# Attention and MLP on one core: five DMA transposes and two sets of masks change their place in the order of the work

## The chip, the cores and the metric

The kernel runs on one core of one Trainium2 chip. The metric is the device time of one execution in microseconds. The kernel before takes 355.95 us (median of three runs, 355.69 to 356.04). The work of each engine is written down in one order by the program, so an edit that only moves lines changes in which order an engine meets its instructions, and what a queue of DMAs issues first.

## The reference

For each of 8 batches and 8 heads, 576 queries attend to 16 beacon keys and to the 576 keys up to their own position (head size 64). The result, with the heads side by side, is x, 576 x 512 per batch. A mixer follows: a low-rank product over the sequence is added to x, and an MLP with ReLU (512 to 2048 to 512) is added to that.

```python
scores = scale * np.matmul(q, k_all.transpose(0, 1, 3, 2))
causal[:, Nb:] = np.triu(np.ones((S, S), dtype=bool), k=1)
a = np.exp(scores - scores.max(-1, keepdims=True))
x = np.matmul(a / a.sum(-1, keepdims=True), v_all)     # heads side by side
h = x.transpose(0, 2, 1) @ U @ V
u = x + h.transpose(0, 2, 1)
out = u + np.maximum(u @ w_ch1, 0.0) @ w_ch2
```

## The kernel before

Batches are counted from 0 in the code: batch 3 is the fourth, batch 5 the sixth. Two heads make a pair, four pairs a batch; pairs are numbered p = 0 to 31, with b = p // 4 the batch and c = p % 4 the pair in it. `P6` is 16, the first pair of batch 4, and `DT0` is 4.

*Attention.* For a pair, TensorE multiplies transposed keys and queries (`kT`, `qT`) into scores in four groups of columns, each a PSUM bank per head (`visit`, line 379 from batch 4 on, line 345 before). ScalarE takes the exponential of each bank into an SBUF tile `expt`. `masks_of` lets VectorE zero what lies above the diagonal: four instructions a pair, lines 321 and 323. `av_unit` then multiplies by the values (line 394) and VectorE divides by the row sums into `xb` (lines 402 and 403). There are eight PSUM banks, taken in the order in which they were given back.

*Transposes.* For batches 0 to 3, TensorE transposes q and k. From batch 4 on, `load_whole(b)` loads them by token with 11 DMAs on GpSimd's queue (line 643, the beacons by line 199), and `turns(b)` makes a list of ten DMA transposes on SyncE's queue (line 655), in the order k0, q0, k1, q1, k2, q2, k3, q3, k4, q4 of the five tiles of tokens. `fill_turns` issues the next n of such a list. `load_batch` loads the values from batch 4 on. The tiles of batch 5 for loaded and for transposed q and k take the places of those of batch 3.

*The mixer and the MLP.* When a batch's `xb` is complete, five DMA transposes write it into `uT` (line 422), also on SyncE's queue; the low-rank product is then added to `uT` by VectorE (line 443). The MLP runs over blocks of 512 rows of `uT`. A block is a queue of 32 layer units of four matmuls each: 16 of the first layer (line 531, emptied by ScalarE in line 544 or VectorE in line 546), then 16 of the second (line 557), of which each fourth ends a tile of 128 rows: VectorE adds the residual (line 570) and SyncE writes the output (line 576). A block's first unit also issues four DMA transposes that bring `uT` back for the residual (line 525). `fill(n)` runs the next n units.

*The order.* The loop at line 988 goes through the pairs. Pairs before 16 interleave fixed lists of scores, values and transposes with units. From p = 16 on, `long_slot` (line 952) writes a pair's order by hand: `go` runs groups of scores of the next pairs, `fill` runs units, `weighted` the values. In this loop the fifth batch's ten transposes are split, five at p = 12 and five at p = 13; the sixth's ten are all at p = 16, behind the transposes of batch 3's `xb`, which `mix_between` issues.

SyncE, like every engine, takes its instructions in order: a DMA that waits holds all behind it.

Of the kernel before, what the change touches and what calls it, by code (L numbers as in the profile page):

```python
# [30 lines left out]
def kernel(  # L31
# [14 lines left out]
    B, H, S, D = q.shape  # L46
# [6 lines left out]
    NH2 = H // 2  # L53
# [9 lines left out]
    NT = NC  # L63
# [563 lines left out]
    def load_batch(b):  # L627
        if b < DT0:
            Ls[b] = qk_tiles()
            emit_loads(b, Ls[b], vss[b % 2])  # L630
        else:
            v_loads(v[b], beacon_v[b], vss[b % 2])

    def load_whole(b):

        Ls[b] = qk_tiles()
        for i, (src, m) in enumerate(((k[b], nk), (q[b], nq))):
            dst = Ls[b][1][i]
            if i == 0:
                beacon_load(nc.gpsimd, beacon_k[b], dst[:, 0, :, :], ALLH)  # L640
            for j in range(NT):
                a = m[j] - nq[j]
                nc.gpsimd.dma_start(  # L643
                    out=dst[a : m[j], j, :, :], in_=src[:, ds(q0[j], nq[j]), :].rearrange("h p d -> p h d")
                )

    def turns(b):

        new_qT(b)
        kn, qn = Ls[b][1]  # L650
        us = []
        for j in range(NT):
            for n, dst, o, m in ((kn, kTs[b % 2], P * j, nk[j]), (qn, qTs[b], q0[j], nq[j])):
                us.append(
                    lambda n=n, dst=dst, o=o, m=m, j=j: nc.sync.dma_start_transpose(  # L655
                        out=dst[:, :, ds(o, m)], in_=n[:m, j, :, :].rearrange("p h d -> p (h d)")
                    )
                )
        return us
# [25 lines left out]
    def regroup_of(p):  # L685
        b, c = divmod(p, NH2)
        prs[p] = [regroup(Ls[b][0], c, i, nc.vector.tensor_copy) for i in range(2)]
# [7 lines left out]
    def new_qT(b):  # L695
        qTs[b] = qkt.tile([P, NH2, S], F16, name="qT", tag="qT")
# [6 lines left out]
    def qkT_of(p):  # L703
        b, c = divmod(p, NH2)
        new_qT_of(p)
        copies = [(act_copy, nc.vector.tensor_copy) if p == 0 else (nc.vector.tensor_copy,)] * 2
        turns = by_heads(Ls[b][0], c)
        for i, t in enumerate(prs.get(p, ())):
            if t is not None:
                turns[i] = in_pair(prs[p])[i]  # L710
        if p == 0:
            turns[0] = beacons_apart(turns[0], Ls[0][0][0], 0)
        return qkT_units(turns, qTs[b], kTs[b % 2], c, copies)
# [4 lines left out]
    def scores_of(p):  # L718
        b, c = divmod(p, NH2)
        return score_units(c, qTs[b], kTs[b % 2], expts_of(p), p < NM)  # L720

    def masks_of(p):
        scores_of(p)[2]()

    def av_of(p):
        b, c = divmod(p, NH2)
        if c == 0:
            xbs[b] = xbp.tile([P, NT, DM], F16, name="xb", tag="xb")
        return [
            lambda i=i: av_unit(b, 2 * c + i, expts[(2 * p + i) % NE], vss[b % 2], xbs[b]) for i in range(2)  # L730
        ]
# [6 lines left out]
    DT0 = 4  # L738
# [11 lines left out]
    def fill_turns(tr, n):  # L750
        for u in tr[:n]:
            u()
        del tr[:n]

    def fill(n):
        while n > 0 and queue:
            u = queue.pop(0)
            if u is not None:
                u()
            n -= 1  # L760
# [28 lines left out]
    with tc.manual_schedule(engines={ENG.PE, ENG.Activation, ENG.DVE, ENG.SP, ENG.Pool}):  # L789
# [93 lines left out]
        for p in range(NH2, NP1):  # L883
            b, c = divmod(p, NH2)
# [36 lines left out]
        tr = []  # L921
# [5 lines left out]
        def mix_between(b):  # L927

            turn, head, parts = mix_units(xbs[b], S * b)
            turn()  # L930
            mixing[:] = [head] + parts
            feed(b)

        def go(parts, mixed=0):

            parts = [(p, g) for p, g in parts if p < NP]
            if parts:
                visit(parts)
            for u in mixing[:mixed]:
                u()  # L940
            del mixing[:mixed]

        def masks_if(p):
            if p < NP:
                masks_of(p)

        def weighted(av, *n):
            for u, m in zip(av, n):
                u()
                fill(m)  # L950

        def long_slot(p, c, av):

            if c == 0:
                go([(p + 1, 0), (p + 1, 1), (p + 1, 2)], 1)
                fill(2)
                weighted(av, 1, 2)
                go([(p + 1, 3), (p + 2, 0), (p + 2, 1)])
            elif c == 1:
                fill(2)  # L960
                masks_of(p)
                fill(1)
                weighted(av, 1, 1)
                go([(p + 1, 2)], 1)
                fill(3)
                go([], 1)
                fill(3)
            elif c == 2:
                go([(p, 3), (p + 1, 0), (p + 1, 1)])
                fill(2)  # L970
                masks_of(p)
                fill(2)
                weighted(av, 1, 1)
                go([(p + 1, 2), (p + 1, 3), (p + 2, 0)])
            else:
                fill(2)
                masks_of(p)
                fill(3)
                go([(p + 1, 1), (p + 1, 2), (p + 1, 3)])
                fill(1)  # L980
                weighted(av, 1, 0)
                if p + 1 < NP:
                    mix_between(p // NH2)
                fill(2)
                masks_if(p + 1)
                fill(1)

        for p in range(NP1, NP):
            b, c = divmod(p, NH2)
            if c == (1 if p >= P6 else 0) and b + 1 < B:  # L990
                load_batch(b + 1)
            if c == 2 and DT0 <= b + 2 < B:
                load_whole(b + 2)
            if c == 0 and b + 1 == DT0:
                tr = turns(b + 1)
            if c == 0 and DT0 < b + 1 < B:
                tr = turns(b + 1)
            sc = scores_of(p + 1) if p < P6 else []
            qk = qkT_of(p + 2) if p + 2 < min(NP, DT0 * NH2) else []
            av = av_of(p) if p < P6 else []  # L1000
            if c == 0 and b + 1 == DT0:
                fill_turns(tr, NT)
            if c == 0 and b > NF and p <= P6:
                (mix if p < P6 else mix_between)(b - 1)
            if c == 1 and b + 1 == DT0:
                fill_turns(tr, NT)
            if c == 0 and b + 1 > DT0:
                fill_turns(tr, 2 * NT)
            if p >= P6:
                long_slot(p, c, av_of(p))  # L1010
                continue
            seq = sc[0:1] + av[0:1] + qk[0:1] + sc[1:3] + qk[1:2] + av[1:2]
            if p + 3 < min(NP, DT0 * NH2):
                seq.append(lambda p=p: regroup_of(p + 3))
            quota = QUOTA.get(b, 9)
            done = 0
            for i, u in enumerate(seq):
                u()
                want = quota * (i + 1) // len(seq)
                fill(want - done)  # L1020
                done = want
# [109 lines left out]
```

## Time and profile before

| | us |
|---|---|
| median of three runs | 355.95 (355.69 to 356.04) |
| the profiled execution | 356.36 |
| its span, first to last instruction | 354.7 |
| TensorE busy | 346.1 (98%) |
| VectorE, ScalarE, GpSimd busy | 188.1, 165.5, 97.5 |
| TensorE waiting for a mask (line 321) | 1.3, in five places |
| TensorE waiting for a DMA transpose | 1.0, in one place |
| granted TensorE clock | 1.00 throughout |

Busy time counts recorded instructions; matmuls are pipelined and their recorded times overlap (379 ns each, started 216 ns apart when nothing holds them), so differences of starts say more than durations. "SPq" is SyncE's queue of DMA issues; a DMA's landing is counted from its issue. `sps` are scores, `po` weighted values, `gps` and `cps` the first and second layer, `ob` an output tile, `ut` the residual, `st` loaded q and k.

### The profile page before, as it was taken

Reading aid. Unit: us, or ns where it says so; the run is one execution under the profiler, and the core shown is the slowest. Engines: PE = TensorE matmul, PEld = TensorE weight load, DVE = VectorE, ACT = ScalarE, POOL = GpSimd, SP = SyncE. Lnnn points to the kernel's source line nnn. Section 1 sums busy time; section 2 is a strip of 40 time slices with the busy share of each in tenths; the row PEclk is TensorE's granted clock in tenths of the full one; section 3 lists DMA queues with packets and bytes.
Section 4 is the critical chain, followed back from the end, with each engine's and each line's share of the span. In section 5 each row is a group of like instructions: output and inputs, shape, how many; then the busy total and the mean of one; then the engine's idle time right before and its main releaser. Section 6 shows DMA issues by size and latency. Waiting matters only on the chain.

```text
span 354.7 us, 7839 instructions
## 1 busy us (share of the span) xinstructions
PE 346.1 (98%) x3110; PEld 174.2 (49%) x3110; DVE 188.1 (53%) x484; ACT 165.5 (47%) x359; POOL 97.5 (27%) x137
## 2 busy tenths in 40 slices
PE   8999999999999999989999999999999999999995
PEld 3665555455544444444544444444445444444443
DVE  5755965678967644634475446435555534313311
ACT  5966851487733664256613862385325202301400
POOL 8956714427447047302740140000000000000000
PEclk9999999999999999999999999999999999999999
DMA  9999999999999939997999798523013413013112
GB/s 182 96 205 172 159 199 172 222 158 125 109 161 147 181 29 120 147 173 126 127 142 182 132 118 123 166 47 68 30 73 77 69 60 104 16 59 98 23 56 71
DMA packets 146636, 41.89 MB, mean 118 GB/s; under 512 B 131488, under 2 KB 142080, under 8 KB 146592
## 3 DMA queue, kind: packets, MB, share of 16 engines
q0 software_dynamic: 87440, 18.18, 67.1%
q1 hardware_dynamic: 58928, 22.84, 36.8%
q8 instruction: 26, 0.43, 0.5%
q10 hardware_dynamic: 224, 0.30, 0.3%
q14 instruction: 18, 0.15, 0.2%
HBM read 37.37 MB, written 9.44 MB: 132 GB/s over the span
## 4 chain that ended last, share of the span: by engine, by line
PE 86%; DMA 5%; DVE 2%; ACT 2%; issue 1%; SPq 1%; POOL 1%; POOLq 0%; DVEq 0%
PE gps L531 33%; PE cps L557 30%; PE po L394 8%; PE sps L345 4%; PE sps L379 3%; DMA st<-in_k_dram 3%; DMA qT<-st 2%; PE tps L274 2%; ACT expt L351 2%; SPq L655 1%; PE idle L249 1%; PE cph L583 1%; PE tps L280 1%; PE qtp L431 1%; POOL vs L217 1%
## 5 line engine op out<-in xcount | busy, mean ns | idle before, releaser
L531 PE MATMUL gps<-uT,w 128*128 128x512 f16 x576 | 136.8, 379 | 0.1
L557 PE MATMUL cps<-w,gT 128*128 128x512 f16 x560 | 130.2, 379 | 0.0
L544 ACT ACTIVATE gT<-gps 128x512 f16<-128x512 f32 x86 | 52.3, 611 | 84.3 <-PE gps L531 82.6
L557 PEld LDWEIGHTS <-gT 128*128 128x128 f16 x560 | 51.0, 98 | 60.7 <-issue 6.6
L531 PEld LDWEIGHTS <-w 128*128 128x128 f16 x576 | 51.4, 98 | 56.4 <-issue 2.2
L385 ACT ACTIVATE expt<-sps 128x496 f16<-128x496 f32 (+2 forms) x120 | 51.6, 537 | 48.5 <-PE sps L379 48.5
L351 ACT ACTIVATE expt<-sps 128x496 f16<-128x496 f32 (+2 forms) x136 | 58.7, 561 | 20.6 <-PE sps L345 20.5
L546 DVE TENSOR_SCALAR gT<-gps 128x512 f16<-128x512 f32 x58 | 40.0, 690 | 49.3 <-PE gps L531 47.7
L570 DVE TENSOR_TENSOR ob<-cps,ut 128x512 f32<-128x512 f32 x31 | 21.4, 690 | 54.1 <-PE cps L557 53.9
L217 POOL DMA_DIRECT2D vs<-in_v_dram x50 | 39.6, 806 | 17.9 <-PE gps L531 5.8
L394 PEld LDWEIGHTS <-expt 128*128 128x128 f16 (+1 forms) x960 | 35.8, 98 | 16.6 <-DVE expt L321 3.8
L394 PE MATMUL po<-vs,expt 128*128 128x65 f16 (+1 forms) x960 | 39.5, 194 | 1.3 <-DVE expt L321 1.3
L403 DVE TENSOR_TENSOR xb<-po,rec 128x320 f16<-128x320 f32 x64 | 31.5, 492 | 2.2
L321 DVE TENSOR_TENSOR expt<-expt,bigmask 128x512 f16<-128x512 f16 x54 | 22.5, 417 | 5.5 <-ACT expt L385 3.1
L402 DVE RECIPROCAL rec<-po 128x5 f32<-128x5 f32 x64 | 12.1, 189 | 23.6 <-PE po L394 23.4
L199 POOL DMA_DIRECT2D vs<-in_beacon_v_dram x8 | 4.3, 539 | 63.4 <-PE po L394 63.4
L345 PE MATMUL sps<-qT,kT 64*128 64x496 f16 (+3 forms) x204 | 18.4, 282 | 0.7 <-DVE qT L307 0.3
L643 POOL DMA_DIRECT2D st<-in_q_dram x20 | 16.9, 865 | 4.4 <-DMA vs<-in_v_dram 2.2
L643 POOL DMA_DIRECT2D st<-in_k_dram x20 | 16.9, 868 | 2.3 <-DMA vs<-in_v_dram 2.3
L443 DVE TENSOR_TENSOR uT<-ups,uT 128x496 f16<-128x496 f32 x24 | 14.5, 667 | 3.1 <-PE ups L456 3.1
L379 PE MATMUL sps<-qT,kT 64*128 64x80 f16 (+2 forms) x180 | 14.8, 281 | 1.0 <-DMA qT<-st 1.0
L307 DVE COPY qT<-tps 128x576 f16<-128x576 f16 (+1 forms) x16 | 11.8, 736 | 4.4 <-PE tps L280 2.3
(95 smaller groups left out, 167.4 us busy)
## 6 DMA issues: line engine op xcount, KB each, us to landing
out_dram<-ob SPq DMA_DIRECT2D x35, 256.0 KB, 2.5
vs<-in_v_dram POOLq DMA_DIRECT2D x18, 128.0 KB, 8.2
w<-in_moe_w_ch_dram POOLq DMA_DIRECT2D x4, 512.0 KB, 6.4
w<-in_moe_w_ch_dram POOLq DMA_DIRECT2D x2, 1024.0 KB, 13.5
st<-in_k_dram POOLq DMA_DIRECT2D x12, 128.0 KB, 8.1
st<-in_q_dram POOLq DMA_DIRECT2D x12, 128.0 KB, 10.7
st<-in_k_dram POOLq DMA_DIRECT2D x2, 576.0 KB, 12.8
st<-in_q_dram POOLq DMA_DIRECT2D x2, 576.0 KB, 16.1
```

Source lines behind the costliest of these rows:

```text
L217: nc.gpsimd.dma_start(out=dst[a : a + nq[j], j, :, :], in_=src[hs, ds(q0[j], nq[j]), :].rearrange("h p d -> p h d"))
L345: nc.tensor.matmul(ps[g, i][:, ds(o, w)], kT[hp, c, ds(P * ch, P)], qT[hp, c, ds(qa, w)], start=not early, stop=True, skip_group_check=early,)
L351: nc.scalar.activation(out=ex[i][:, ds(SLOT * g, gw[g])], in_=ps[g, i][:, 0 : gw[g]], func=AF.Exp, scale=scale)
L379: nc.tensor.matmul(ps[p, g, i][:, ds(o, w)], kT[hp, c, ds(P * ch, P)], qT[hp, c, ds(qa, w)], start=True, stop=True,)
L385: nc.scalar.activation(out=at[p][3][i][:, ds(SLOT * g, gw[g])], in_=ps[p, g, i][:, 0 : gw[g]], func=AF.Exp, scale=scale)
L394: nc.tensor.matmul(po[:, j, :], ex[0 : nk[c], ds(blk[(c, j)], P)], vs[0 : nk[c], ds(c * H * E + h * E, E)], start=(c == 0), stop=(c == j),)
L403: nc.vector.tensor_tensor(out=xb[:, :, ds(h * D, D)], in0=po[:, :, 0:D], in1=r.broadcast_to([P, NT, D]), op=ALU.mult)
L531: nc.tensor.matmul(g[:, 0:n], w1[:, cc, ts(dc, P)], uT[:, cc, ds(t0, n)], start=(cc == 0), stop=(cc == NCC - 1))
L544: nc.scalar.activation(out=gT["t"][:, dc, 0:n], in_=g[:, 0:n], func=AF.Relu)
L546: nc.vector.tensor_scalar_max(out=gT["t"][:, dc, 0:n], in0=g[:, 0:n], scalar1=0.0)
L557: nc.tensor.matmul(ps[:m, :], gT["t"][:, dc, ds(P * i, m)], w2[:, dc, :], start=(dc == 0), stop=turned and dc == NDC - 1, skip_group_check ...
L643: nc.gpsimd.dma_start(out=dst[a : m[j], j, :, :], in_=src[:, ds(q0[j], nq[j]), :].rearrange("h p d -> p h d"))
```

## The change

Four things change their place; no instruction is added, removed or altered.

- `turns(5)`, the sixth batch's transposes, is made at p = 15 (c = 3, b = 3). Its first five (k0, q0, k1, q1, k2) are issued there, ahead of the pair's other work and so ahead of batch 3's `xb` transposes at p = 16. The other five stay at p = 16 behind them.
- `load_whole(5)` is called at p = 13 and not at p = 14.
- In `long_slot`, for c = 1 and c = 2, the pair's masks stand behind one layer unit and not behind two; the unit passed follows the masks. This touches p = 17, 18, 21, 22, 25, 26, 29 and 30.
- The fifth batch's transposes and those of batches 6 and 7 keep their places; their conditions are only written in another way.

```diff
             elif c == 1:
+                fill(1)
+                masks_of(p)
                 fill(2)
-                masks_of(p)
-                fill(1)
                 weighted(av, 1, 1)
...
             elif c == 2:
                 go([(p, 3), (p + 1, 0), (p + 1, 1)])
-                fill(2)
+                fill(1)
                 masks_of(p)
-                fill(2)
+                fill(3)
                 weighted(av, 1, 1)
...
-            if c == 2 and DT0 <= b + 2 < B:
+            if c == (1 if b + 1 == DT0 else 2) and DT0 <= b + 2 < B:
                 load_whole(b + 2)
-            if c == 0 and b + 1 == DT0:
-                tr = turns(b + 1)
-            if c == 0 and DT0 < b + 1 < B:
-                tr = turns(b + 1)
...
-            if c == 0 and b + 1 == DT0:
+            if c == 0 and DT0 <= b + 1 < B and b != DT0:
+                tr = turns(b + 1)
+            if c == NH2 - 1 and b + 1 == DT0:
+                tr = turns(b + 2)
+            if c in (0, NH2 - 1) and b + 1 == DT0:
                 fill_turns(tr, NT)
             if c == 0 and b > NF and p <= P6:
                 (mix if p < P6 else mix_between)(b - 1)
-            if c == 1 and b + 1 == DT0:
-                fill_turns(tr, NT)
-            if c == 0 and b + 1 > DT0:
+            if c == 1 and b + 1 == DT0 or c == 0 and b >= DT0:
                 fill_turns(tr, 2 * NT)
```

## The prediction

> **What bounds the kernel now.** I read the page first, for the busiest engine, then the list of who waited for whom on TensorE, then TensorE's instructions in order of time from the fifth batch on, and last the queues that stand behind the two waits found there.
>
> ```profile
> PE 346.1 (98%) x3110; PEld 174.2 (49%) x3110; DVE 188.1 (53%) x484; ACT 165.5 (47%) x359; POOL 97.5 (27%) x137
> ```
> TensorE is busy for 98% of the span. No other engine passes 53%, so an edit that issues the same matmuls can gain only what TensorE stands still. Its list of waits is short:
> ```profile
> PE po L394 <- DVE expt L321: 1.3, 5, 0.3
> PE sps L379 <- DMA qT<-st: 1.0, 1, 1.0
> ```
> (columns: total us, times, longest). The first is the weighted values waiting for a mask, the second the scores waiting for a transposed query tile. Asked by stretches, four of the five mask waits lie at 140.6, 178.5, 215.2 and 251.9 us, one in each second pair (c = 1) of batches 4 to 7; the fifth is before 130 us, in code the diff leaves alone. The transpose wait is at 157.75 us. TensorE's order of time, fourth batch's end and later:
> ```profile
> 130.54 0.79 PE L379 MATMUL sps<-qT,kT 64*128 64x496 f16 x10
> 137.61 2.76 PE L557 MATMUL cps<-w,gT 128*128 128x512 f16 x12
> 140.63 0.63 PE L394 MATMUL po<-vs,expt 128*128 128x65 f16 x15 [0.25 <-DVE expt L321]
> 150.05 2.76 PE L557 MATMUL cps<-w,gT 128*128 128x512 f16 x12
> 152.65 1.03 PE L531 MATMUL gps<-uT,w 128*128 128x512 f16 x4
> 157.75 0.39 PE L379 MATMUL sps<-qT,kT 64*128 64x496 f16 x2 [1.02 <-DMA qT<-st]
> 168.44 0.79 PE L379 MATMUL sps<-qT,kT 64*128 64x496 f16 x10
> 205.15 0.79 PE L379 MATMUL sps<-qT,kT 64*128 64x496 f16 x10
> ```
> The reader should compare starts, because recorded matmuls overlap. Twelve cps matmuls that run on freely take 152.65 - 150.05 = 2.60 us; before the mask wait they take 140.63 - 137.61 = 3.02, so that wait really costs 0.42 and not 0.25. One batch lasts 168.44 - 130.54 = 37.90 us where the transpose wait falls, and 205.15 - 168.44 = 36.71 in the next, with the same work: the transpose wait costs 1.19. Now SyncE's queue, which issues every transpose and every output:
> ```profile
> 117.50 5.79 SPq L525 DMA_TRANSPOSE ut<-uT  x4
> 129.80 7.29 SPq L422 DMA_TRANSPOSE uT<-xb  x5
> 137.27 1.22 SPq L655 DMA_TRANSPOSE kT<-st  x1
> 148.55 1.36 SPq L655 DMA_TRANSPOSE qT<-st  x1
> 153.77 1.98 SPq L576 DMA_DIRECT2D out_dram<-ob  x4
> ```
> From 129.80 it issues 15 transposes end to end: five of the fourth batch's x, ten of the sixth batch's q and k. The eighth of those ten, the query tile that the wait at 157.75 needs, goes out at 148.55 and lands 8.9 us later, at 157.4. Ahead of this the queue has nothing to issue from 123.3 to 129.8, and neither have the DMA engines; in the 40 slices of 123 to 137 us (0.35 us each) the zeros run from 124.1 to 130.0:
> ```profile
> DMA  9970000000000000000016049999999999999999
> ```
> For the masks, what VectorE does:
> ```profile
> 139.55 0.69 DVE L570 TENSOR_TENSOR ob<-cps,ut 128x512 f32<-128x512 f32 x1 [3.44 <-PE cps L557]
> 140.16 0.41 DVE L321 TENSOR_TENSOR expt<-expt,bigmask 128x512 f16<-128x512 f16 x1
> ```
> It idles 3.44 us, empties an MLP result, and only then masks; yet the exponentials that the masks read start at 137.31 and, two of 341 ns each, are done by 138.0.
>
> **The change part by part.** *Five transposes earlier.* Keys and queries of tiles 0 and 1 and keys of tile 2 of the sixth batch are issued from p = 15, between the ut transposes (end 123.3) and x (129.80). What they read was issued by GpSimd at 103.8 to 112.7 and landed 3.3 to 9.1 us later, at the latest near 120.5. What they overwrite is last read by scores at about 117. So they start at 123.4. Their issue cost there is bounded by 1.30 us each (the spacing at 210.98 to 217.5, when little else moved) and 1.65 each (16.5 us for ten from 137.27 to 153.77): 6.5 to 8.25 us, end 129.9 to 131.6. I take 1.30, the row with idle DMA engines: x starts 0.1 us late; at the other end, 1.8. Behind x stand five transposes and not ten: the wanted query tile is third, issued near 141 and landing by 151.5 with the longest landing of this stretch (9.6). Its matmul will be wanted at 157.75 - 1.02 - 0.42 = 156.3. The 1.19 goes. Next late would be the last tile, wanted at 162.5; it landed at 159.2 even before. The four outputs, at 153.77 now, go out as their tiles are ready (the last near 153.5), and the ut transposes at 156.12 follow a little sooner.
>
> *Who waits for x.* It is added by VectorE from 144.12. The fourth x transpose lands near 142.6, so 1.1 us of delay are free even after the mask gain. Then the four adds (end 146.54) fill the slack until scores need their banks at 149.45: 2.9 us more. Up to 4.0 us late, x costs nothing; 1.8 is within this.
>
> *Load of the sixth batch one pair sooner* (11 DMAs on GpSimd's queue, one beacon, ten of tokens). Cost 0 and gain 0: nothing else is issued on that queue between the two places, and it already started at 103.78, when a wait of 5.3 us for the last copy out of the old tile ended. If that cover went, it would be later, never past the 123.4 that needs it. The second five of the fifth batch's transposes keep their place.
>
> *Masks at c = 1* (four instructions on VectorE, four batches): they pass the emptying at 139.55. They can start at 138.0 and take 0.9 us (140.16 to 141.05 now), done at 138.9, before the matmuls of that emptying end at 139.5, so nothing behind them on VectorE is held. The weighted values at 140.2 find them done: 4 x 0.42 = 1.68. Lower bound 4 x 0.25 = 1.0, the wait as the profile states it; I take the starts, since the free run of twelve is the same instruction. *Masks at c = 2* (another four batches): at 150.12 they already follow the exponentials after 0.74 us of idleness, ahead of the next emptying (152.85), and TensorE has no gap there (2.60 us for twelve). Nothing gained or lost.
>
> Sum: 1.19 + 1.68 = 2.87 us. The profiled execution took 356.36 (span 354.70 and 1.66 around it), 0.41 above the median of the runs; it would come to 353.5. From the median, 355.95 - 2.87 = 353.1.
>
> [...]
>
> **Rivals.** (1) *Only one half pays.* If the masks are replaced as the last wait by something else at 140.2, such as a bank not empty, only 1.19 comes: 354.8. For it: nothing shows what is second. Against: the scores' banks popped next are empty at 138. If the query tile is late all the same, only 1.68 comes: 354.3. Against: 4.8 us of margin. (2) *The change does nothing that can be measured:* both waits turn into others of their length, 355.95; against it stands the next batch, which runs without the transpose wait in 36.71. (3) *Slower: x is held by the five.* Should they start not at 123.4 but only when the fourth batch's values are done (129.8), by a wait that I don't see, x starts 7.3 to 8.25 late; beyond 4.0 each microsecond is lost on TensorE at 149, so 3.3 to 4.25 against 2.87 saved: 356.4 to 357.3. It decides only from x some 7.6 us late on (4.0 + 2.87 + 0.7). Against: all that the five read and overwrite is ready before 121.
>
> **How the numbers follow.** Two tenths of a per cent, 0.7 us, is what a measurement of this kernel can tell from no change (three runs lie within 0.35). Both halves pay: 0.68, at 353.1, its own range 352.6 to 353.9 (the waits' stated lengths, 2.05, at the upper end; spread of runs at the lower). One half: 0.15, 354.3 or 354.8. Nothing: 0.07. Slower: 0.10, at 356.9; the ring rule holds half of that chance. So faster 0.83, same 0.07, slower 0.10, and 352.6 to 355.0 holds the first two cases.
>
> **What would show it.** Right: TensorE's list without the wait for query tiles and with one mask wait left; five line 655 transposes on SyncE from about 123.4; the eighth query or key transpose near 141; the stretch from 130.5 about 36.3 us long, and each later batch as well; masks at about 138.0, ahead of the emptying. Wrong: x first issued after 133, line 443 waiting for a DMA, or a new wait ahead of the weighted values at 140.2.

## The result and the profile after

The changed kernel takes 353.56 us (median of six runs, 353.20 to 353.86) against 355.91 (355.68 to 356.06) for the kernel before: a ratio of 0.9934, 95% interval 0.9922 to 0.9947. That is faster by 0.66%, or 2.35 us; 353.1 was predicted. A second measurement (`changed_again`, below) gave 0.9919 (0.9889 to 0.9949). The profiled execution took 353.56 us with a span of 351.9.

TensorE is busy for 345.3 us, where it was 346.1, and the span lost 2.8 (354.7 to 351.9). Of these the listed waits lost 2.0; the other 0.8 had been recorded as busy. Twelve matmuls are recorded with 2.76 us though the next starts after 2.60 where nothing holds it, and this 0.16 counts as busy ahead of each of the five waits that went. TensorE's list of waits (total us, times, longest) after:

```profile
PE idle L249 <- DVE ones L153: 1.2, 1, 1.2
PE sps L345 <- DVE qT L307: 0.3, 1, 0.3
PE po L394 <- DVE expt L321: 0.3, 1, 0.3
PE sps L337 <- ACT expt L351: 0.2, 1, 0.2
PE sps L345 <- DVE uT L443: 0.2, 1, 0.2
```

The wait for a transposed query tile is gone and of the five waits for a mask one is left, the early one that the diff does not touch. Nothing new came in. By stretches, each from the first scores of a batch's first pair to those of the next batch (columns: length, then busy us of TensorE, its weight loads, VectorE, ScalarE, GpSimd, then granted clock, DMA share, GB/s):

```profile
130.67:166.94 36.27, 36.27 (x325) 17.84 (x325) 18.03 (x45) 19.08 (x42) 14.51 (x19) 1.00 1.48 128
166.94:203.21 36.27, 36.27 (x325) 17.85 (x325) 20.35 (x53) 18.63 (x41) 13.64 (x18) 1.00 1.56 145
...
```

Three batches now last the same, 36.27, 36.27 and 36.28 us, and TensorE is busy through all of it. Before they lasted 37.90, 36.71 and 36.70. The first lost 1.63 (1.19 + 0.42 were forecast), the others 0.44 and 0.42.

SyncE's queue after:

```profile
123.24 1.19 SPq L655 DMA_TRANSPOSE kT<-st  x1
...
128.88 1.19 SPq L655 DMA_TRANSPOSE kT<-st  x1
130.17 7.14 SPq L422 DMA_TRANSPOSE uT<-xb  x5
...
140.46 1.31 SPq L655 DMA_TRANSPOSE qT<-st  x1
```

The five fill the gap that stood there from 123.3 to 129.8. The first landed after 2.4 us and the fifth after 3.1. x starts 0.37 us later than before (TensorE, too, is 0.13 later there in this execution: 130.67 and not 130.54). The wanted query tile is the last line: issued at 140.46 and not 148.55, it lands 7.4 us later, at 147.9, some 8 us before its matmul.

TensorE and VectorE around the masks of pair 17, in order of time:

```profile
137.74 2.76 PE L557 MATMUL cps<-w,gT 128*128 128x512 f16 x12
140.34 0.61 PE L394 MATMUL po<-vs,expt 128*128 128x65 f16 x15
...
155.95 0.69 PE L379 MATMUL sps<-qT,kT 64*128 64x336 f16 x10
```
```profile
137.81 0.43 DVE L321 TENSOR_TENSOR expt<-expt,bigmask 128x512 f16<-128x512 f16 x1 [1.58 <-ACT expt L385]
...
139.67 0.69 DVE L570 TENSOR_TENSOR ob<-cps,ut 128x512 f32<-128x512 f32 x1 [0.88 <-PE cps L557]
```

Twelve cps matmuls now take 140.34 - 137.74 = 2.60 us ahead of the weighted values, the free run. VectorE masks as soon as the exponentials are there, and stands 0.88 us before the emptying that the masks used to follow. At 155.95 the ten score matmuls run on in one piece; before, eight ran and two waited.

### The profile page after: what moved, and what is told of

Same layout as the page of the kernel before. It is cut to its first block, busy times and chain, and to the rows that moved or that the text cites. A ratio compares the mean times of both kernels' runs of the same rounds, so it can differ in the third digit from the quotient of the medians.

```text
span 351.9 us, 7841 instructions
## 1 busy us (share of the span) xinstructions
PE 345.3 (98%) x3110; PEld 174.5 (50%) x3110; DVE 188.3 (54%) x484; ACT 165.3 (47%) x359; POOL 97.8 (28%) x137
## 4 chain that ended last, share of the span: by engine, by line
PE 94%; ACT 2%; DVE 1%; DMA 1%; issue 0%; DVEq 0%
PE gps L531 36%; PE cps L557 35%; PE po L394 9%; PE sps L345 4%; PE sps L379 4%; PE tps L274 2%; ACT expt L351 2%; PE cph L583 1%; DMA stq<-in_q_dram 1%; PE tps L280 1%; PE qtp L431 1%; PE sps L337 1%; PE ups L456 1%; PE ups L410 1%; PE qtp L486 0%
```

## The experiments

### Each half alone

Only the masks of the second pairs, in the kernel before:

```diff
             elif c == 1:
-                fill(2)
+                fill(1)
                 masks_of(p)
-                fill(1)
+                fill(2)
```

> The kernel before with one edit: in the second pair of each batch from the fifth on (c = 1) the masks stand behind one layer unit, not two. Theory on record: VectorE masks ahead of the emptying of the output tile, four gaps of 0.42 us on TensorE go, 1.68 us in all, ratio 0.9953; the wait of 1.0 us for the query tile at 157 us stays or grows, because TensorE comes to it 0.42 us sooner (then only 1.26 us net, ratio 0.9965: the query tile lands at a time that SyncE's queue sets, and not TensorE). Rival: another wait takes the place of the masks at 140.2 us, ratio 1.000.

Measured: 355.15 us against 356.34 before on that chip, by medians a ratio of 0.9967; over the single executions 0.9981 (0.9962 to 0.9999), a wide interval because a few executions of both lie 2 to 3 us above the rest. In the trace the gaps of 0.42 are gone, and the wait for the query tile stays:

```profile
137.37 2.76 PE L557 MATMUL cps<-w,gT 128*128 128x512 f16 x12
139.97 0.61 PE L394 MATMUL po<-vs,expt 128*128 128x65 f16 x15
...
155.58 0.48 PE L379 MATMUL sps<-qT,kT 64*128 64x336 f16 x8
156.65 0.39 PE L379 MATMUL sps<-qT,kT 64*128 64x496 f16 x2 [0.60 <-DMA qT<-st]
```

So the net is nearer to 1.26 than to 1.68 us (1.19 by the medians, at most 1.35 by the interval). That fits the forecast: TensorE comes to the query tile sooner, but the tile comes when SyncE's queue brings it, so that the first of the four mask gaps is paid for nothing unless the transposes move as well. The trace by itself does not show this. The tile landed some 1.1 us sooner in this execution than in the one before the change (147.81 + 8.5 = 156.3, not 148.55 + 8.9 = 157.4), and the wait was shorter, not longer.

Only the transposes, in the kernel before (loads and masks as they were): the diff's conditions on `turns` and `fill_turns` alone.

> The kernel before with one edit: the sixth batch's first five q and k transposes are issued one pair sooner, ahead of the fourth batch's x; masks and loads as before. Theory on record: the wait of 1.02 us for the query tile goes, 1.19 us by the starts of the matmuls, ratio 0.9967; the four mask waits of 0.25 us stay. Rival (x held by the five): line 443 waits for x and the ratio is 1.000 or above.

Measured: 355.10 us, ratio 0.9969 (0.9959 to 0.9979), 1.1 us, as forecast. TensorE's list (same columns):

```profile
PE po L394 <- DVE expt L321: 1.3, 5, 0.3
...
```

All five mask waits are there, and none for a query tile. The loads are at their old place here, and the five transposes start at 122.95 all the same: they did not need the loads one pair sooner. In the kernel before they stood behind x's transposes, issued from 129.80 on, and the first of them started at 137.27.

### The edits that were costed at nothing

The load one pair sooner and the masks of the third pairs, in the kernel before:

```diff
-            if c == 2 and DT0 <= b + 2 < B:
+            if c == (1 if b + 1 == DT0 else 2) and DT0 <= b + 2 < B:
...
             elif c == 2:
-                fill(2)
+                fill(1)
                 masks_of(p)
-                fill(2)
+                fill(3)
```

> The kernel before with the two edits that were costed at nothing: the sixth batch's q and k loaded one pair sooner, and the masks of the third pair (c = 2) behind one layer unit. Theory on record: ratio 1.000 within 0.1%, GpSimd's loads start at 103.8 us as before and the masks of pair 18 at 150.1. Rival: the loads or the masks do move, ratio 0.997 or 1.003.

Measured: 356.31 us against 356.34, ratio 0.9996 (0.9973 to 1.0019), with both waits in the trace. The loads start at 103.21 and the masks of pair 18 at 149.54, each some 0.58 sooner than before, but so do TensorE's scores in this execution (155.67, not 156.25): neither moved. It is also one more execution of the old order: here the query tile's wait was 0.65 us and not 1.02. In the starts it cost 1.45 - 0.62 = 0.83 (the ten scores to the next matmul, 155.67 to 157.12, against 0.62 in a free run); with the masks alone it was 1.39 - 0.62 = 0.77, in the execution that the prediction was worked out from 1.20.

### How many transposes must go ahead, and how many may

The changed kernel with one, seven, nine or ten ahead of x, and not five (the one line that differs, for ten):

```diff
             if c in (0, NH2 - 1) and b + 1 == DT0:
-                fill_turns(tr, NT)
+                fill_turns(tr, NT if c == 0 else 10)
```

> The changed kernel with one of the sixth batch's ten transposes ahead of the fourth batch's x, not five. The wanted query tile is then seventh behind x, and not eighth (before) or third (changed). One transpose takes 1.45 us of SyncE's queue, so the tile lands near 155.6 us, and its matmul is wanted near 156.1: half a microsecond of margin. Theory (the length of the queue ahead of the tile is the whole cause, and its landing varies from run to run): no wait in most executions, time within 0.15% of the changed kernel, ratio 0.993 to 0.9945, but a wider spread than its 353.1 to 354.5. Rival (the five must go ahead together, because x's landings hold the tile): the wait stays at 0.8 us or more, ratio 0.9965, as with the masks alone.

One: 353.23 us, ratio 0.9911 (0.9897 to 0.9925). No wait for the tile is left in the trace; the scores at 155.70 run in one piece of ten. One transpose ahead does what five do. The tile is issued at 147.03 and lands 8.1 us later, at 155.1, some 2.3 us sooner than in the kernel before: 1.5 by its place in SyncE's queue and 0.8 by a shorter landing. A wider spread had been expected; in five runs it was not wider (353.02 to 353.58).

> The changed kernel with seven of the sixth batch's ten transposes ahead of the fourth batch's x, not five: x is issued from about 132.8 us on, 2.6 us later. Theory on record (x is free up to 4.0 us late): same time as the changed kernel within 0.1%, VectorE's first add moves from 143.8 to about 145.7 and TensorE shows no wait at 149. Rival (every late x costs): 2 us more than the changed kernel.

Seven: 353.77 us, ratio 0.9926 (0.9898 to 0.9955), against 353.32 for the changed kernel on the same chip: 0.45 or 0.13% more by the medians, which the times alone do not tell from nothing. In the trace x is issued at 132.92, VectorE's first add runs at 146.50, and TensorE shows no named wait. But six score matmuls are drawn out:

```profile
148.95 1.37 PE L379 MATMUL sps<-qT,kT 64*128 64x208 f16 x6
150.25 2.76 PE L557 MATMUL cps<-w,gT 128*128 128x512 f16 x12
```

They take 1.30 us from start to start and 0.60 in the changed kernel. So 0.70 us is lost with x 3.1 us later than in the kernel before, where the prediction still held it free. VectorE's four adds end at 148.92, the emptying behind them (line 570) at 149.52, and the one behind that, which adds the last columns of x, at 149.92:

```profile
149.44 0.48 DVE L443 TENSOR_TENSOR uT<-uend,uT 128x320 f16<-128x320 f32 x1
```

Taken one by one, the fifth and the sixth of the score matmuls start at 149.57 and 149.97, each 0.05 us behind the end of one of those two emptyings; with nine it is 151.72 and 152.12, again 0.05 behind. So they wait for the banks of these two, though the list of waits names no such wait.

> The changed kernel with all ten of the sixth batch's q and k transposes ahead of the fourth batch's x, not five. It measures how late x may come. x would be issued from 137 us on, 7 us later than in the changed kernel. Theory on record (x is free up to 4.0 us late, then TensorE loses each microsecond, because the scores at 149 us need the banks that VectorE empties after x): 3.2 us over the changed kernel, ratio 1.002 to the kernel before. Rival (only the first layer's matmuls at 152.4 us wait for x): about 1 us over the changed kernel, ratio 0.996. [...]

> As before with nine ahead: x is issued from about 135.5 us on, 5.3 us later than in the changed kernel and 1.4 us sooner than with ten. With ten, TensorE stood 3.06 us for VectorE's adds and 0.6 more behind, and then ran at a granted clock of 0.50 for some 6 us. Theory A (the clock falls only after a stand of about 3 us): here the stand is 1.7 us, the clock stays at 1.00, and the kernel is about 2.3 us over the changed one, ratio 1.000. Theory B (any stand of over 1 us lowers the clock): 4 to 5 us over the changed one, ratio 1.005 to 1.008.

Ten: 360.43 us, ratio 1.0113 (1.0088 to 1.0137). Nine: 357.47 us, ratio 1.0030 (1.0002 to 1.0057). Both are slower than the kernel before, nine only just. TensorE's order with ten, and then with nine:

```profile
151.91 0.25 PE L379 MATMUL sps<-qT,kT 64*128 64x208 f16 x1 [3.06 <-DVE uT L443]
152.50 0.33 PE L379 MATMUL sps<-qT,kT 64*128 64x208 f16 x1 [0.34 <-DVE uT L443]
153.08 2.12 PE L379 MATMUL sps<-qT,kT 64*128 64x496 f16 x4 [0.25 <-DVE uT L443]
155.12 4.83 PE L557 MATMUL cps<-w,gT 128*128 128x512 f16 x12
```
```profile
149.38 0.25 PE L379 MATMUL sps<-qT,kT 64*128 64x208 f16 x1 [0.46 <-DVE uT L443]
...
151.13 1.54 PE L379 MATMUL sps<-qT,kT 64*128 64x496 f16 x3 [0.21 <-DVE uT L443]
152.60 5.30 PE L557 MATMUL cps<-w,gT 128*128 128x512 f16 x12
```

VectorE with ten:

```profile
151.19 2.41 DVE L443 TENSOR_TENSOR uT<-ups,uT 128x496 f16<-128x496 f32 x4 [8.52 <-DMA uT<-xb]
...
154.12 0.48 DVE L443 TENSOR_TENSOR uT<-uend,uT 128x320 f16<-128x320 f32 x1
```

With ten, the six score matmuls wait one after the other for VectorE to add x into `uT` and so to empty the banks they need. The listed waits sum to 3.65 us, near the 3.2 that was forecast, but the list leaves out the last ones: the sixth score starts at 154.65, 0.05 behind VectorE's last emptying (154.12 + 0.48), and the cps matmuls start at 155.12. In the changed kernel they start 149.75 - 146.46 = 3.29 us behind the twelve cps ahead of the scores, which here makes 146.10 + 3.29 = 149.39. So the banks cost 5.7 us and not 3.65. And the twelve cps matmuls behind them take 159.80 - 155.12 = 4.68 us and not 2.60. The granted clock tells why. By stretches, with ten (the number ahead of the last two is the clock), and then with nine:

```profile
148.80:151.90 3.10, 0.05 (x1) 0.08 (x1) 0.71 (x2) 0.00 (x0) 0.00 (x0) 1.00 2.34 158
...
155.10:157.50 2.40, 2.40 (x7) 0.89 (x7) 0.98 (x5) 0.80 (x2) 0.00 (x0) 0.50 0.63 217
...
159.80:163.00 3.20, 3.20 (x42) 1.98 (x41) 2.17 (x5) 0.60 (x1) 0.00 (x0) 1.00 0.41 123
```
```profile
151.00:152.00 1.00, 0.73 (x2) 0.20 (x2) 1.00 (x4) 0.91 (x2) 0.00 (x0) 0.63 0.85 160
...
156.00:157.00 1.00, 1.00 (x4) 0.45 (x3) 0.00 (x0) 0.00 (x0) 0.00 (x0) 0.50 0.35 131
```

With ten the clock is at 0.50 from about 152.5 to 159.3, with nine from about 151.3 to 158.1. From where the scores would have started (with ten 146.10 + 2.69 = 148.79, by the 149.15 - 146.46 of the changed kernel) to the first-layer matmul (159.80) it takes 11.0 us with ten, and 3.2 in the changed kernel. Of the 7.8 more, 5.7 is what the banks cost and 2.1 the halved clock in the twelve cps matmuls; up to 0.2 of the 5.7 may be the clock, too, since the last score takes 0.47 us up to the cps and with seven 0.28. With nine the cps matmuls start at 152.60 and not at 146.17 + 3.29 = 149.46, 3.1 later, though the listed waits sum to 1.34.

Theory A fell: with nine the clock fell although no listed wait is over 0.46 us. Of nine's ten executions, four had a mean clock of 0.997 to 1.000 and took 356.1 to 356.6 us; the other six, at 0.988 to 0.995, took 357.4 to 359.6. So whether the clock falls differs from execution to execution, and theory B, by which any such stand lowers it, does not hold either, though its 4 to 5 us over the changed kernel met the median (357.47 - 353.32 = 4.15). Where the clock held, nine took 2.8 to 3.2 us over the changed kernel's 353.32 on that chip; A expected 2.3, and the 3.1 that the banks cost in the trace agrees.

### What the masks wait behind

The changed kernel with the masks of the second pairs behind all three units:

```diff
             elif c == 1:
-                fill(1)
+                fill(3)
                 masks_of(p)
-                fill(2)
```

> The changed kernel with the masks of the second pairs (c = 1) behind all three layer units, one unit later than in the kernel before. Theory: what counts is the emptying of the output tile ahead of the masks on VectorE, and not the number of units: the third unit empties nothing, so the four gaps are 0.42 us again, as with two units, and the kernel is 1.68 us over the changed one, ratio 0.998. Rival: the gap grows by the matmuls of one unit, 0.86 us each, 5 us over the changed one, ratio 1.007.

Measured: 355.23 us, ratio 0.9967 (0.9947 to 0.9987), 1.9 us over the changed kernel at 353.32. The trace has the old gap and not a longer one, 141.30 - 138.29 = 3.01 us for twelve:

```profile
138.29 2.76 PE L557 MATMUL cps<-w,gT 128*128 128x512 f16 x12
141.30 0.63 PE L394 MATMUL po<-vs,expt 128*128 128x65 f16 x15 [0.25 <-DVE expt L321]
```

A unit that empties nothing takes no place in VectorE's order. What the edit did was to bring the masks ahead of one instruction, the emptying in line 570.

> The changed kernel itself, on one chip with the next three. The trace of before had the query tile's wait at 1.19 us, 0.41 us above its median; in two other executions with the old order of transposes the same wait cost 0.77 and 0.83. Theory now: the median wait is near 0.8, so both halves give 0.8 + 1.68 = 2.5 us, ratio 0.993, and the runs lie closer together than those of the kernel before, because only the wait for the tile varies. Theory on record: 2.87 us, ratio 0.992.

Measured: 353.32 us against 356.17, ratio 0.9919 (0.9889 to 0.9949), 2.85 us (1.8 to 4.0). That is the 2.87 on record rather than the 2.5 of the newer theory, but the interval holds both. By the difference to `masks_third` the masks are worth 1.9 us, by `turns_only` the transposes 1.1: 3.0 together.

## Why the prediction was right

*Direction, mechanism and range.* Both waits went, nothing took their place, and 353.56 lies in the range, and in the likeliest case's own range of 352.6 to 353.9. The first measurement of the gain, 2.35 us (interval 1.9 to 2.8), is short of the forecast 2.87; the second, 2.85, is on it.

*The transposes' term.* Forecast 1.19, measured 1.1 (0.7 to 1.5) alone. The step "the transpose wait costs 1.19" took one execution for the kernel. Two other executions with the old order cost 0.77 and 0.83, so that one reading was a draw from a spread, and the prediction's range takes it down only to the 1.02 that the list states. That the first execution was 0.41 us over the median does not mend it: 1.19 - 0.41 = 0.78 looks like the other two, but the execution of `load_and_c2` was 0.59 under its median, and by the same correction its 0.83 would become 1.42. The 0.7 to 1.5 of `turns_only` holds 0.78 and 1.19 alike. How close 1.19 came to the mean is in part luck.

*The masks' term.* 1.68 by the starts of the matmuls, and not the 1.0 that the list of waits says, was right: 36.71 and 36.70 became 36.27 and 36.28, about 4 x 0.43 = 1.72, and by times it was 1.9. The other wait of the first rival did not appear.

*The costs put at nothing.* The load and the masks of the third pairs did nothing that can be measured: ratio 0.9996 (0.9973 to 1.0019). The five transposes ran at 1.30 us of spacing but for one gap of 0.53, so x was 0.37 us late and not 0.1, within its slack.

*What was wrong, without weight on the time.* "Up to 4.0 us late, x costs nothing" was too generous: with seven ahead, 3.1 us late, 0.7 is already lost. The slack of 2.9 us ran from the end of the fourth add (146.54) to the scores at 149.45. But six scores take the banks of six emptyings, and the last of these ends at 147.53 in the kernel before:

```profile
147.05 0.48 DVE L443 TENSOR_TENSOR uT<-uend,uT 128x320 f16<-128x320 f32 x1
```

With seven ahead, VectorE's first add runs 16.03 us behind the scores at 130.47, and in the changed kernel 13.14 behind those at 130.67: it is 2.89 late and 0.70 is lost, so the slack is 2.2. x's own five issues also took 8.00 us there and not 7.29. Beyond the slack each microsecond is lost, as the prediction says: with ten the add is 7.74 late (151.19 - 130.31 - 13.14), which makes 5.5, against the 5.7 by the starts. And the rival in which the five hold x was priced at 356.4 to 357.3 for x 7.3 to 8.25 us late. With ten, 7.2 us late, it is 360.4: the price had the slack too long and left out the clock. No run shows the ring rule, to which the prediction gave half of the 0.10 for slower: the five landed after 2.4 to 3.1 us, the fifth at 132.0 while x was still being issued, and x's own landings took 4.7 to 8.7 us, 4.7 to 9.0 before.

## What to carry to other kernels

Where a DMA is late, count the places in the queue that issues it before looking at its transfer: one place, in a gap that the queue had anyway, was enough for all of the wait (with one ahead the tile was issued 1.5 us sooner; the wait had cost 1.20). To move an instruction, count the instructions of its engine that it passes, not the units written between: with the masks behind three units the twelve matmuls ahead of the weighted values took 3.01 us, behind two 3.02, and 2.60 once the masks had passed the one emptying on VectorE. The length of a wait should be taken from starts, since the list can put it too low (0.25 for 0.42 us at the masks, 3.65 for 5.7 with ten ahead) or leave it out (0.70 with seven), and a wait that was read in one execution should be read in others as well: here the same one cost 1.20, 0.83 and 0.77 us.

## What the runs showed of the hardware

With ten transposes ahead, TensorE lost more than it stood: banks that came 5.7 us late were followed by a granted clock of 0.50 up to 159.3, which cost another 2.1, and all four executions had a mean clock of 0.995 or less. With nine, where six scores had to wait for their banks for 3.1 us in all and no listed wait was over 0.46, six of ten executions had a mean clock under 0.996. The other four, of the same kernel, had 0.997 to 1.000. No length of a single wait that lowers the clock follows from this: the longest listed wait was 3.06 us with ten and 0.46 with nine, and in the kernel before a wait of 1.02 us left the clock at 1.00 in its trace.

The kernel before may lose its clock at times, too. Of 85 executions with all ten transposes behind x whose clock is on record (the kernel before on three chips, `masks_c1` and `load_and_c2`), six had a mean clock of 0.992 to 0.995, and they are the slowest of their runs, at 357.0 to 359.3 us. Of 45 with one, five or seven ahead none is under 0.997. Whether the wait for the query tile has a part in this, so that the change saves it as well, is not shown: no trace of such an execution was taken.
